# Gated attention with a token mixer: the accumulating stores taken out, four adds put on GpSimd, a clear put on VectorE, and a PSUM bank taken later

## The chip, the core and the metric

The kernel runs on one core of a Trainium2 chip. The core has a matrix engine (TensorE, in the rows PE, with its weight loads as PEld), three engines for elementwise work (VectorE, DVE in the rows; ScalarE, ACT; GpSimd, POOL), and a queue engine (SyncE, SP) that issues most transfers between HBM and the on-chip memory. GpSimd can issue transfers too. Matrix products go into PSUM, which has eight banks of 128 partitions by 512 fp32 numbers; everything else on the chip is in SBUF. The engines run side by side, each in the order of its own instructions, and wait for each other through semaphores.

The metric is the device time of one execution in microseconds (us). The kernel before takes 1622.77 us, the median of three runs (1622.52 to 1623.23).

## The reference

The input x has 2048 tokens of 512 numbers. It is normalised, and two branches work on the result, which are multiplied and added to x:

```python
xn = _layernorm(x)
s = attention(xn, wqkv, wo)          # 32 heads of 16, softmax over all 2048 tokens, then @ wo
g = silu(mixer(xn, w1, b1, w2, b2))  # layernorm, then an MLP across tokens: 2048 -> 1792 -> 2048, gelu
return x + s * g
```

All of it is fp32. A number is split into an upper and a lower part, and a product is made of three matrix products (upper by upper, upper by lower, lower by upper).

## The kernel before, in words

The tokens are 16 blocks (`b`) of 128. The kernel first normalises x and makes queries, keys and values; then comes the long middle part, in which the attention of one pair of heads after another goes through TensorE (scores, then exponentials on ScalarE, then the products with the values), while the maxima of the next pair's scores are found on VectorE. In the same loop stands a second stream of products, the filling: first all products of the mixer, then those of the output projection with `wo`. A step of the loop has an `s`; from `s = NU = 512` on there are no more maxima, and only scores, values and filling remain. The last heads end shortly before the end of the program, and the projection of the blocks 8 to 15 needs them, so it is completed after the loop.

**The filling.** A generator yields one product after another, and `take(n, each)` asks it for `n` of them and hands each to `each`. A generator step that begins a block also takes a PSUM bank for it (`ps_sc.hold("dn")`), and one that begins a quarter of a mixer weight also issues the weight's load and its split into two parts (`w_load`, `w_split`, on SP and GpSimd). After its `n` products, `take` looks at the next thing in the stream with `fill.peek()`, to see whether a block has ended. Looking at it makes it: the bank is taken, or the load and the split are issued, at this place in the program. The blocks 12 and 13 (`LATE` and the one after) are interleaved by three products each while `n < ND - 2`, so their banks are asked for in the same place.

**Banks.** Up to `s = 512` the scores have four banks (`ps_sc`), those of the maxima three (`ps_mx`). From then on all seven form one row: a tile takes the bank at the front and puts it to the back, a held bank leaves the row until it is given back. The scores of a step that follow each other take the row's banks in turn, and a score has to wait until the exponential that reads its bank is done.

**The last half of the blocks.** For each block from 8 on, the part of the projection that does not need the last heads is multiplied by g and added to x before the loop ends (`part`, then `store_y`). The result lies in HBM until the end: blocks 10 to 13 in the buffer `y_d`, from which `load_second` reads it back into `ys[b]`. The blocks 8 and 9 (`SUMMED`) are stored straight to the output.

**The end of the program.** After the loop, the last heads' numerators are turned by TensorE, divided on VectorE into `apart[0]` (a buffer that `clear_apart` sets to zero at `s = NU + 16`) and turned back. Then eight blocks are completed in the order 8, 9, 12, 13, 10, 11, 14, 15, which the code counts as `n = 0` to `7`. `product(n)` makes three matrix products; `gated(n)` multiplies them by g on VectorE; `added(i, eng)` adds `ys` and issues the store on SP. For the blocks 8 and 9 `added` issues an accumulating transfer on GpSimd's queue instead (`accum_op=OP.add`), which adds to what lies in the output. The dictionary `adding` says after which `n` each `added` stands. Block 15 goes by halves (`in_parts`).

Blocks 0 to 7 were completed before, inside the loop, by `finish` on VectorE.

Of the kernel before, what the change touches and what calls it, by code (L numbers as in the profile page):

```python
# [12 lines left out]
OP = mybir.AluOpType  # L13
# [9 lines left out]
def tile_attention_token_mixer(ctx, tc, x, wqkv, wo, w1, b1, w2, b2, out):  # L23
    nc = tc.nc
    P = 128
# [5 lines left out]
    NB = S // P  # L31
# [835 lines left out]
    apart = []  # L867

    def clear_apart():

        apart.append(el.tile([P, 2, 512], F32, name="uo"))
        nc.gpsimd.memset(apart[0], 0.0)

    xts = {}
    gts = {}
# [1 line left out]
    gates = {}  # L877
    held = []
    PARTS = NB - 2
    LATE = NB - 4  # L880
    HALVES = 5
    SUMMED = range(NB // 2, NB // 2 + 2)

    def load_part(b):

# [23 lines left out]
        after(2, two)  # L909

    def store_y(b, y):
        if b in SUMMED:
            nc.sync.dma_start(out[b * P : (b + 1) * P, :], y)
            return
        nc.sync.dma_start(y_d[b], y)
        if b >= NB // 2:
            unkept.append(b)
# [3 lines left out]
    def load_second():  # L921

        b = next((b for b in unkept if b >= PARTS), min(unkept))
        unkept.remove(b)
        i = b - NB // 2
        while len(held) < NB // 8:
            held.append(big.tile([P, S], F32, name="big"))
        ys[b] = held[i // 4][:, i % 4 * 512 : i % 4 * 512 + 512]
        nc.sync.dma_start(ys[b], y_d[b] if b < PARTS else xv[:, b, :])
# [110 lines left out]
    def everything():  # L1040
        yield from mixer()
        yield from rest()

    class Fill:
# [10 lines left out]
        def next(self):  # L1055
            x = self.peek()
            self.ahead.clear()
            return x

    fill = Fill(everything())  # L1060
    open_ = True
# [7 lines left out]
    def take(n, each):  # L1069

        nonlocal open_, done
        got = 0
        while open_ and (got < n or fill.peek() and len(fill.peek()) == 2):
            x = fill.next()
            if x is False:
                open_ = False
            elif x is None:
                break
            elif len(x) == 2:
                def then(empty, back):  # L1080
                    empty()
                    back()

                each(None, lambda x=x: then(*x))
                if fill.peek() is None:
                    fill.next()
                    break
            else:
                each(x, None)
                got += 1  # L1090
        done += got

    def whole(x, then):
# [279 lines left out]
    for c in range(2):  # L1373
        for a in range(2):
            j = 2 * a + c
            nc.vector.tensor_tensor(
                out=spread[:, c, :, 96 + DH * a : 112 + DH * a], in0=turned[:, :, j, DH * a : DH * a + DH],
# [12 lines left out]
    def lower(h, c):  # L1390
        o = oc[ND - 1, 2 + c][96:, :, 256 * h : 256 * h + 256]
        sub(nc.vector, o[:, 1, :], back[h, c][96:, :256], o[:, 0, :])
# [17 lines left out]

    def added(n, eng):
        b = half[n]
        if b in SUMMED:
            nc.gpsimd.dma_start(out[b * P : (b + 1) * P, :], gates[b], accum_op=OP.add)
            return
        eng.tensor_tensor(out=gates[b], in0=ys[b], in1=gates[b], op=OP.add)
        nc.sync.dma_start(out[b * P : (b + 1) * P, :], gates[b])

# [18 lines left out]
        turn_back(1, c)  # L1437
        upper(1, c)
    lower(1, 0)
    adding = {0: [0], 1: [1], 3: [2], 4: [3], 5: [4], 6: [5, 6]}  # L1440
    for n in range(8):
        if n > 5:
            some(len(beside) if n == 7 else len(beside) - 9)
        product(n)
        if n == 7:
            in_parts(n)
            break
        gated(n)
        for i in adding.get(n, ()):
            added(i, nc.gpsimd if i in () else nc.vector)  # L1450
        if n == 1:
            lower(1, 1)

# [26 lines left out]
```

## Time and profile before

| | us |
|---|---|
| median of three runs | 1622.77 |
| the profiled execution | 1621.93 |
| its span, from the first to the last instruction | 1620.0 |
| TensorE busy (11,899 products) | 1610.4 |
| VectorE busy | 1414.3 |
| ScalarE busy | 1192.3 |
| GpSimd busy | 552.4 |

The profile is of one execution. A row of the timeline has the start in us from the span's start, the duration in us, the engine, the line of the kernel, the operation, the tiles (written <- read), the shapes, how often, and in brackets the idle time of the engine before it with what ended it. A row of the windows has a stretch, and for each engine the busy time and in brackets the number of instructions, then the granted TensorE clock, the busy share of the DMA engines and the GB/s that they moved. A row of the chain of waits has a start, a duration and the work that the end of the program hung on at that time. A busy TensorE is not necessarily at its peak, since its products are pipelined: products of 512 columns follow each other every 0.23 us though each row shows 0.39.

### The profile page before, as it was taken

To read this page: it belongs to the slowest core of one execution; us is meant where nothing else is said; L and a number is where in the kernel's file an instruction comes from. 1 tells how busy PE (TensorE), PEld (TensorE's weight loads), DVE (VectorE), ACT (ScalarE), POOL (GpSimd) and SP (SyncE) were. 2 spreads that over 40 slices of the span, in tenths; PEclk is the share of its full clock that TensorE was granted. 3 is DMA by queue.
4 is the path that set the end of the run, shared out by engine and by line. 5 is a ranking of instruction groups with operands and counts; after the bars stand their busy time and mean duration, and the time that the engine had idled before them with its cause. 6 is when DMAs were issued, how large, how long until landed. Compare 5 with 4: busy or idle time off the path is not lost.

```text
span 1620.0 us, 31089 instructions
## 1 busy us (share of the span) xinstructions
PE 1610.4 (99%) x11899; PEld 876.2 (54%) x11899; DVE 1414.3 (87%) x2478; ACT 1192.3 (74%) x2306; POOL 552.4 (34%) x651
## 2 busy tenths in 40 slices
PE   9999999999999999999999999999999999999998
PEld 8888854554555554554454554544555545554544
DVE  7665999999999999999999999999999999999945
ACT  3333477777777777777877787777877777888885
POOL 1224844342244332332333332223232322563330
PEclk9999999999999999999999999999999999999999
DMA  7478441515133141826151522304150614444346
GB/s 231 178 249 200 120 93 41 96 39 78 41 68 75 27 79 40 241 71 109 41 83 37 85 59 42 69 31 76 38 86 31 113 32 80 112 99 131 111 136 222
DMA packets 151120, 153.34 MB, mean 95 GB/s; under 512 B 51372, under 2 KB 109996, under 8 KB 147900
## 3 DMA queue, kind: packets, MB, share of 16 engines
q1 hardware_dynamic: 146524, 150.25, 38.6%
q0 software_dynamic: 4448, 1.12, 0.5%
q8 instruction: 93, 1.52, 0.4%
q14 instruction: 55, 0.45, 0.1%
HBM read 99.63 MB, written 50.58 MB: 93 GB/s over the span
## 4 chain that ended last, share of the span: by engine, by line
PE 97%; DVE 1%; POOL 0%; issue 0%; ACT 0%; DMA 0%; SPq 0%; POOLq 0%; DVEq 0%
PE av L987 31%; PE dn L1132 23%; PE sc L971 17%; PE mx L533 14%; PE sc L436 3%; PE dn L672 2%; PE mx L436 2%; DVE mxp L537 1%; PE av L436 1%; PE dn L1178 0%; PE sc L104 0%; PE sc L102 0%; PE sc L103 0%; PE mx L340 0%; PE mx L102 0%; PE mx L104 0%
## 5 line engine op out<-in xcount | busy, mean ns | idle before, releaser
L537 DVE TENSOR_REDUCE mxp<-mx 128x1 f32<-128x512 f32 x2026 | 1250.3, 682 | 112.0 <-PE mx L533 85.7
L976 ACT ACTIVATE prob<-sc 128x512 f32<-128x512 f32 x2004 | 1039.7, 607 | 282.3 <-PE sc L971 116.5
L533 PE MATMUL mx<-big 48*128 48x512 f32 x2026 | 769.5, 419 | 0.1
L971 PE MATMUL sc<-big 50*128 50x512 f32 x2004 | 733.6, 412 | 0.5 <-ACT prob L976 0.5
L987 PE MATMUL av<-prob,vp 128*32 128x512 f32 x4096 | 545.5, 604 | 0.3 <-DVE ev L723 0.2
L1132 PE MATMUL dn<-hu,wh 64*128 64x512 f32 x1520 | 506.2, 404 | 0.0
L971 PEld LDWEIGHTS sc<-big 50*128 50x128 f32 x2004 | 353.9, 186 | 230.4 <-ACT prob L976 205.6
L533 PEld LDWEIGHTS mx<-big 48*128 48x128 f32 x2026 | 356.7, 185 | 196.0 <-DVE mxp L537 173.8
L1132 PEld LDWEIGHTS dn<-hu,wh 64*128 64x128 f32 x1520 | 272.1, 184 | 68.2 <-issue 45.3
L1132 PE MATMUL dn<-hu,wl 64*128 64x512 f32 x762 | 301.9, 396 | 0.0
L987 PEld LDWEIGHTS av<-prob,vp 128*32 128x32 f32 x4096 | 80.9, 108 | 176.3 <-issue 164.0
L95 POOL TENSOR_TENSOR wl<-raw,wh 128x512 fp32r<-128x512 f32 x124 | 150.7, 1218 | 64.0 <-ACT wh L167 22.6
L165 POOL CAST wh<-raw 128x512 fp32r<-128x512 f32 x104 | 60.4, 581 | 277.0 <-PE dn L1132 114.5
L1132 PEld LDWEIGHTS dn<-hu,wl 64*128 64x128 f32 x762 | 140.5, 184 | 11.6
L561 POOL CAST m<-f 16x128 fp32r<-16x128 f32 x31 | 8.7, 280 | 240.7 <-DVE f L549 240.7
L99 POOL DMA_DIRECT2D big<-m x124 | 65.6, 536 | 0.0
L622 POOL TENSOR_TENSOR sq<-u 128x512 f32<-128x512 f32 x11 | 11.5, 1041 | 133.7 <-ACT u L616 133.7
L1132 PE MATMUL dn<-wh,hu 64*128 64x512 f32 x144 | 51.0, 407 | 0.0
L709 POOL TENSOR_SCALAR t<-t 128x512 f32<-128x512 f32 x16 | 23.8, 1488 | 79.6 <-ACT t L706 79.5
L436 PE MATMUL sc<-xt,big 128*128 128x512 f32 x184 | 44.5, 390 | 0.0
L95 POOL TENSOR_TENSOR hu<-hx,hu 128x512 fp32r<-128x512 f32 x16 | 20.4, 1294 | 68.5 <-ACT hu L279 68.5
L672 PE MATMUL dn<-hu,wh 64*128 64x512 f32 x128 | 42.3, 392 | 0.0
(224 smaller groups left out, 1180.6 us busy)
## 6 DMA issues: line engine op xcount, KB each, us to landing
raw<-in_B_w_dram SPq DMA_DIRECT2D x104, 256.0 KB
big<-k_d SPq DMA_DIRECT2D x96, 128.0 KB
big<-q_d SPq DMA_DIRECT2D x96, 128.0 KB
q_d<-sg SPq DMA_DIRECT2D x16, 512.0 KB
k_d<-sg SPq DMA_DIRECT2D x16, 512.0 KB
num_d<-ev SPq DMA_DIRECT2D x30, 256.0 KB
u_d<-uo SPq DMA_DIRECT2D x14, 512.0 KB
hu<-u_d SPq DMA_DIRECT2D x14, 512.0 KB
```

The lines of the kernel that those rows point to most:

```text
L95: eng.tensor_tensor(out=o, in0=a, in1=b.bitcast(F32), op=OP.subtract)
L99: queue.dma_start(dst.bitcast(F32), src.bitcast(F32))
L165: nc.gpsimd.tensor_copy(whs[n][:, :m, :], raws[n][:, :m, :])
L436: nc.tensor.matmul(ps, w[part][:, kd, m], xt[kd][:, z, :], start=w is wh and z == 0 and kd == 0, stop=w is wl and kd == ND - 1,)
L533: nc.tensor.matmul(ps, q[o : o + 48, r * P : (r + 1) * P], k[o : o + 48, c * 512 : (c + 1) * 512], start=True, stop=True,)
L537: nc.vector.tensor_reduce(mxp[u // 16][:, a, r % 8, c : c + 1], ps, axis=AX.X, op=OP.max)
L672: nc.tensor.matmul(ps, w(slice(0, 64)), m(slice(0, 64)), start=first, stop=last)
L709: nc.gpsimd.tensor_scalar(t, t, 1.0, None, op0=OP.add)
L971: nc.tensor.matmul(ps, ks[p][o : o + 50, kb * P : (kb + 1) * P], qs[p][o : o + 50, at : at + 512], start=True, stop=True,)
L976: nc.scalar.activation(e, ps, AF.Exp, scale=scale)
L987: nc.tensor.matmul(av[32 * j : 32 * j + 32, :], vps[p][:, kb, 16 * a : 16 * a + 32], prob.pop((t, a, c)), start=kb == 0, stop=kb == NB - 1,)
L1132: made.append(lambda r=r, start=first and a == lead, stop=last and a != lead: nc.tensor.matmul(ps, w(r), m(r), start=start, stop=stop,))
```

## The change

It has five pieces.

1. `SUMMED` goes. The blocks 8 and 9 are stored to `y_d` and read back like the blocks 10 to 13, and there are no more accumulating transfers.
2. `added` for `n = 0` to `3` (blocks 8, 9, 12 and 13) is done by GpSimd, the rest by VectorE, and the adds stand at other places.
3. The clear of `apart[0]` is done by VectorE.
4. `take` looks at the next thing in the stream only behind the last product of a block (`x[4]` is the mark of the last product). Otherwise a bank is taken, and a weight's load and split are issued, in the next call of `take`, with the first product that they are for.
5. `while not held or ...` gives the same number of buffers as before at this size.

```diff
     def clear_apart():
         apart.append(el.tile([P, 2, 512], F32, name="uo"))
-        nc.gpsimd.memset(apart[0], 0.0)
+        nc.vector.memset(apart[0], 0.0)
...
-    SUMMED = range(NB // 2, NB // 2 + 2)
...
     def store_y(b, y):
-        if b in SUMMED:
-            nc.sync.dma_start(out[b * P : (b + 1) * P, :], y)
-            return
         nc.sync.dma_start(y_d[b], y)
         if b >= NB // 2:
             unkept.append(b)
...
-        while len(held) < NB // 8:
+        while not held or len(held) < NB // 8:
...
         got = 0
-        while open_ and (got < n or fill.peek() and len(fill.peek()) == 2):
+        ended = False
+        while open_ and (got < n or ended and fill.peek() and len(fill.peek()) == 2):
             x = fill.next()
...
             else:
                 each(x, None)
                 got += 1
+                ended = x[4]
...
     def added(n, eng):
         b = half[n]
-        if b in SUMMED:
-            nc.gpsimd.dma_start(out[b * P : (b + 1) * P, :], gates[b], accum_op=OP.add)
-            return
         eng.tensor_tensor(out=gates[b], in0=ys[b], in1=gates[b], op=OP.add)
         nc.sync.dma_start(out[b * P : (b + 1) * P, :], gates[b])
...
-    adding = {0: [0], 1: [1], 3: [2], 4: [3], 5: [4], 6: [5, 6]}
+    adding = {0: [0], 1: [1], 2: [2], 3: [3], 5: [4, 5], 6: [6]}
...
         for i in adding.get(n, ()):
-            added(i, nc.gpsimd if i in () else nc.vector)
+            added(i, nc.gpsimd if i < 4 else nc.vector)
```

What this does to the order of the instructions is seen at three places. The lines of the changed kernel have slightly smaller numbers: L1407 is the multiply that was L1409, L1411 the add that was L1416, L1418 and L1419 the halves of block 15.

VectorE at the end of the program, before, from the multiply of block 12 on (`prob<-sc` and `prob<-dn` are the multiplies, `prob<-big` the adds):

```order
L1409 TENSOR_TENSOR prob<-sc,hu 128x512 x2
L1416 TENSOR_TENSOR prob<-big,prob 128x512
L1409 TENSOR_TENSOR prob<-sc,hu 128x512
L1416 TENSOR_TENSOR prob<-big,prob 128x512
L1409 TENSOR_TENSOR prob<-sc,hu 128x512
L1416 TENSOR_TENSOR prob<-big,prob 128x512
L1409 TENSOR_TENSOR prob<-dn,hu 128x512
L1416 TENSOR_TENSOR prob<-big,prob 128x512 x2
L1423 TENSOR_TENSOR prob<-dn,hu 128x256
L1424 TENSOR_TENSOR prob<-big,prob 128x256
```

And in the changed kernel:

```order
L1407 TENSOR_TENSOR prob<-sc,hu 128x512 x4
L1411 TENSOR_TENSOR prob<-big,prob 128x512 x2
L1407 TENSOR_TENSOR prob<-dn,hu 128x512
L1411 TENSOR_TENSOR prob<-big,prob 128x512
L1418 TENSOR_TENSOR prob<-dn,hu 128x256
L1419 TENSOR_TENSOR prob<-big,prob 128x256
```

VectorE has five adds before and three after; the four multiplies of blocks 12, 13, 10 and 11 now follow each other.

GpSimd at the end of the program, the changed kernel's difference:

```order
-L905 TENSOR_TENSOR t<-t,xt 128x512 x3
-L872 MEMSET uo 128x1024
-L1414 DMA out_dram<-prob 128x512 x2
-L1476 UNCONDITIONAL_BRANCH
-L1476 ISA
+L904 TENSOR_TENSOR t<-t,xt 128x512 x3
+L1411 TENSOR_TENSOR prob<-big,prob 128x512 x4
+L1471 UNCONDITIONAL_BRANCH
+L1471 ISA
```

The clear has gone to VectorE (it stands there between the completions of blocks 3 and 4), and four adds stand where two accumulating transfers stood.

TensorE at the first products of block 13, two rounds of scores behind `s = 512`, before, with the tiles' numbers, which count up in the order in which tiles are taken. `sc` are scores, `dn_22597` is the bank of block 12 and `dn_22598` that of block 13:

```order
L971 MATMUL sc_22660<-big_1481,big_1482 128x512
L1178 MATMUL dn_22597<-wh_20255,hu_20596 128x512
L971 MATMUL sc_22665<-big_1481,big_1482 128x512
L1178 MATMUL dn_22597<-wl_20256,hu_20596 128x512
L1178 MATMUL dn_22598<-wh_20255,hu_20596 128x512
L1178 MATMUL dn_22597<-wh_20255,hu_20596 128x512
L1178 MATMUL dn_22598<-wl_20256,hu_20596 128x512
```

And in the changed kernel, where the two banks are `dn_22599` and `dn_22661`:

```order
L967 MATMUL sc_22662<-big_1481,big_1482 128x512
L1176 MATMUL dn_22599<-wh_20255,hu_20596 128x512
L967 MATMUL sc_22667<-big_1481,big_1482 128x512
L1176 MATMUL dn_22599<-wl_20256,hu_20596 128x512
L1176 MATMUL dn_22661<-wh_20255,hu_20596 128x512
L1176 MATMUL dn_22599<-wh_20255,hu_20596 128x512
L1176 MATMUL dn_22661<-wl_20256,hu_20596 128x512
```

The products stand in the same order. Block 13's bank is taken right behind block 12's before (22597, 22598), ahead of the second and the third score at `s = 512`, and two rounds later in the changed kernel, next to the score beside its own first product (22661, 22662).

In the middle part the same piece of the change moves some weight splits on GpSimd and loads on SP a few rows down, behind the small transfers of the maxima or the stores of g; on TensorE, VectorE and ScalarE the middle part's instructions stand as they stood.

## The prediction

> **What bounds the kernel now.** I read the windows first, for each stretch the busy time of the five engines.
>
> ```profile
> 20.00:1400.00 1380.00, 1379.93 (x10249) 756.37 (x10247) 1227.32 (x2144) 1008.48 (x1946) 467.34 (x560) 1.00 0.37 85
> ...
> 1560.00:1600.00 40.00, 39.83 (x296) 16.31 (x295) 14.98 (x24) 36.72 (x74) 3.45 (x3) 1.00 0.70 230
> ...
> 1606.00:1613.00 7.00, 6.61 (x30) 5.13 (x28) 6.87 (x12) 0.00 (x0) 1.86 (x2) 1.00 0.32 55
> ```
>
> TensorE (first number behind the length) has no gap in the middle part, 1379.93 of 1380.00 us, and almost none up to 1600 us. In the last stretch VectorE (third) is as full, 6.87 of 7.00. The chain of waits says who hands over to whom at the end:
>
> ```profile
> 1605.34 0.71 PE av L1403 x3
> 1606.07 0.72 DVE prob L1409 x2
> ...
> 1615.19 0.43 DVE prob L1424
> ```
>
> From 1606.07 us the end hangs on VectorE alone, up to the last half of block 15 at 1615.62. Behind it lie 4.4 us of transfer and closing. So the change can gain in two places: a stall of TensorE ahead of 1606 us, or the 14 us behind it. It can lose nearly anywhere that TensorE is made to wait.
>
> **The middle part: nothing.** TensorE, VectorE and ScalarE keep their order there; what moves is the split of some weight quarters on GpSimd, and loads on SP.
>
> ```profile
> POOL wh L165 <- PE dn L1132: 114.5, 16, 13.6
> ...
> L95 POOL TENSOR_TENSOR wl<-raw,wh 128x512 fp32r<-128x512 f32 x124 | 150.7, 1218 | 64.0 <-ACT wh L167 22.6
> ```
>
> The split mostly waits for TensorE to give a buffer back, up to 13.6 us; it is early, not late, and TensorE's list of waits names no split. A split that comes some rows later, behind a 0.3 us cast and four small transfers, uses up some of this. TensorE has no idle time to win and no wait on GpSimd, so I take 0, with 0.3 us either way for the range; if that cover were gone, each late split would cost TensorE up to its 1.2 us.
>
> **The bank: -0.4 us.** At `s = 512` TensorE stands still once:
>
> ```profile
> 1550.39 0.50 PE L971 MATMUL sc<-big 50*128 50x512 f32 x1 [0.49 <-ACT prob L976]
> ...
> 1549.74 1.78 ACT L976 ACTIVATE prob<-sc 128x512 f32<-128x512 f32 x3 [0.58 <-PE sc L971]
> ...
> 1548.75 0.68 DVE L898 TENSOR_TENSOR t<-dn,gt 128x512 f32<-128x512 f32 x1
> ```
>
> Blocks 12 and 13 both hold one of the scores' four banks, so the third score needs the bank of the first, whose exponential has just begun (1549.74). With block 13's bank still in the row, the second score goes to that bank, which VectorE had read by 1549.43, and the third to one that is free. All 0.49 us go at best. The fourth score then takes the first one's bank, free at about 1550.35, 0.1 us later than it could start, so I take 0.4; the lower end is 0, if another wait takes its place. From there to 1600 us TensorE is the fuller engine (39.83 of 40.00 against ScalarE's 36.72), so what is won here arrives at the end.
>
> **Stores and loads of blocks 8 and 9: nothing.** The two stores go to `y_d` in place of the output, and two loads of 256 KB come on SP. SP works in order, and the load of block 9 must wait until its store, issued at 1536.96, has landed.
>
> ```profile
> 1536.96 0.45 SPq L913 DMA_DIRECT2D out_dram<-t  x1
> ...
> 1549.44 0.34 SPq L889 DMA_DIRECT2D xt<-in_A_x_dram  x1
> ```
>
> The next entry in the queue goes out 12 us later for a reason of its own (the buffer it fills is in use). A store takes about 2 us to land (below), so the queue is free again by 1540.
>
> **The clear on VectorE: nothing.** It stands between the completions of blocks 3 and 4.
>
> ```profile
> 1579.58 0.95 POOL L872 MEMSET uo<- 128x1024 f32 x1
> ...
> 1590.12 0.69 DVE L956 TENSOR_TENSOR t<-hu,t 128x512 f32<-128x512 f32 x1
> 1591.70 0.69 DVE L955 TENSOR_TENSOR t<-dn,hu 128x512 f32<-128x512 f32 x1 [0.89 <-PE dn L1178]
> ```
>
> VectorE idles 0.89 us at that place and again before each following block. A clear of 1024 columns costs it between 0.95 (GpSimd's) and 1.4 us (twice a 512-column operation); block 4's completion is up to 0.5 us late and the next gap takes it up. Nobody waits for that bank at once, since seven go round.
>
> **The adds: +0.3 us on VectorE.** This is its end:
>
> ```profile
> 1607.94 1.29 DVE L1409 TENSOR_TENSOR prob<-sc,hu 128x512 f32<-128x512 f32 x2
> ...
> 1612.14 0.69 DVE L1409 TENSOR_TENSOR prob<-dn,hu 128x512 f32<-128x512 f32 x1
> 1612.74 1.29 DVE L1416 TENSOR_TENSOR prob<-big,prob 128x512 f32<-128x512 f32 x2
> 1613.94 0.42 DVE L1423 TENSOR_TENSOR prob<-dn,hu 128x256 f32<-128x256 f32 x1
> ...
> 1609.05 0.39 PE L1403 MATMUL sc<-wh,hu 128*128 128x512 f32 x1
> ...
> 1611.32 0.39 PE L1403 MATMUL dn<-wh,hu 128*128 128x512 f32 x1
> ...
> 1612.22 0.39 PE L1403 MATMUL dn<-wh,hu 128*128 128x512 f32 x1
> ```
>
> Operations of 512 columns follow each other every 0.60 us (1612.14, 1612.74), and from block 15's first half to the end it is 1.68 us (1613.94 to 1615.62). All times in this part are those of the profile, ahead of the 0.4. If nothing is in the way, the multiplies start at 1607.94, 1608.54, 1609.14 and 1609.74 (block 11's product is ready at 1609.44), the two adds at 1610.34 and 1610.94, block 14's multiply at 1611.75 (TensorE is done at 1611.71), its add at 1612.35, the halves at 1612.95. The end is 1614.63, 0.99 us earlier.
>
> But GpSimd adds at the same time, and such pairs are in the trace:
>
> ```profile
> 14.58 1.29 POOL L95 TENSOR_TENSOR big<-wh,big 128x512 fp32r<-128x512 f32 x1
> 15.62 0.81 DVE L95 TENSOR_TENSOR big<-wl,big 128x512 fp32r<-128x512 f32 x1
> 16.34 0.68 DVE L95 TENSOR_TENSOR big<-raw,big 128x512 fp32r<-128x512 f32 x1
> ...
> 1551.38 1.28 POOL L95 TENSOR_TENSOR hu<-sq,hu 96x512 fp32r<-96x512 f32 x1
> 1552.63 1.26 POOL L905 TENSOR_TENSOR t<-t,xt 128x512 f32<-128x512 f32 x1
> ...
> 1551.87 2.11 DVE L561 CAST m<-f 16x128 fp32r<-16x128 f32 x1
> ...
> 1548.13 1.28 POOL L905 TENSOR_TENSOR t<-t,xt 128x512 f32<-128x512 f32 x1
> 1548.75 0.68 DVE L898 TENSOR_TENSOR t<-dn,gt 128x512 f32<-128x512 f32 x1
> ...
> 1574.76 1.28 POOL L905 TENSOR_TENSOR t<-t,xt 128x512 f32<-128x512 f32 x1 [20.87 <-DVE t L898]
> ```
>
> A multiply with one input in PSUM and one in SBUF is not disturbed (0.68 beside GpSimd). A VectorE operation with both inputs in SBUF that began inside GpSimd's took 0.81, and its follower started 0.47 us after GpSimd's end (14.58 + 1.29 = 15.87; 16.34). A small cast was held for 2.11 us, through two GpSimd operations, to 1553.98. So the two adds of blocks 10 and 11, whose inputs are both in SBUF, are likely held. GpSimd's adds take 1.25 us each in a row (1551.38, 1552.63) and start 0.1 us after VectorE's result (the last row: VectorE's operation ended at 1574.69). Block 8's multiply ends at 1606.07 + 0.69 = 1606.76, so they end at 1606.84 + 3 x 1.25 + 1.28 = 1611.87. Block 10's add, wanted at 1610.34, waits for that; block 11's starts at 1612.34, and the rest follows by 0.60: 1612.94, 1613.54, halves 1614.14, end 1615.82, 0.2 later than before. If VectorE slips in between GpSimd's third and fourth add, block 11's add waits for the fourth, and the end is 1615.72. If GpSimd's adds stand 1.36 apart, it is 1616.15. I take +0.3 from bounds of -0.99 and +0.5, nearer the upper, since the cast's row shows a hold through two operations.
>
> A rule of the Trainium skill bears on this (SBUF — State Buffer, section Who interferes with whom): a VectorE instruction with two SBUF inputs and a GpSimd instruction that reads SBUF exclude each other, the one that comes first has the port for all its length, and one SBUF input doesn't contend. The row of 0.81 alone would say 0.13 us for each held add, thus -0.99 + 0.26 = -0.73 and 1620.4 in the end; by the rule the add stands still until GpSimd is done. No row has two GpSimd adds against two VectorE adds, so the trace agrees only in part.
>
> **The end of the transfers: -1.2 us.**
>
> ```profile
> 1609.85 4.81 SPq L1417 DMA_DIRECT2D out_dram<-prob  x5
> ...
> L1425 SPq DMA_DIRECT2D out_dram<-prob x2: 606/845/1084, 1614.8 to 1616.0; - x2
> ...
> 1610.01 1.86 POOL L1414 DMA_DIRECT2D out_dram<-prob  x2 [29.47 <-DVE prob L1416]
> ...
> 1610.40:1611.50 1.10, 1.10 (x6) 0.93 (x5) 1.10 (x3) 0.00 (x0) 1.10 (x2) 1.00 0.65 238
> 1611.50:1616.60 5.10, 1.11 (x5) 0.57 (x4) 4.05 (x9) 0.00 (x0) 0.37 (x1) 1.00 1.06 222
> 1616.60:1618.40 1.80, 0.00 (x0) 0.00 (x0) 0.00 (x0) 0.00 (x0) 0.00 (x0) 0.77 1.02 381
> 1618.40:1618.70 0.30, 0.00 (x0) 0.00 (x0) 0.00 (x0) 0.00 (x0) 0.00 (x0) 0.50 0.28 92
> 1618.70:1620.00 1.30, 0.00 (x0) 0.00 (x0) 0.00 (x0) 0.00 (x0) 0.00 (x0) 0.50 0.00 0
> ```
>
> The first store, issued at 1609.85, moves alone: 238 GB/s over 1.1 us are its 262 KB, landed by 1611.6, 1.75 us after its issue. Then the DMA engines are full (1.06) at only 222 GB/s while the accumulating transfers run, against 381 GB/s in the 1.8 us after them. The first half of block 15 takes 1.08 us to issue, so the second, ready at 1615.62, is issued at 1616.03 and lands by 1618.7, 2.65 later. Without the accumulating transfers (issued from 1610.01) the stores start 1.7 us earlier (GpSimd's first add ends at 1608.12), and most come further apart than the 0.69 us that 262 KB take at 381 GB/s. So the last should be issued at once, 0.03 behind VectorE as the first half is (-0.35), and land in 1.75 (-0.9). I take 1.2; the bounds are 0 and -1.3.
>
> The sum is 0 - 0.4 + 0 + 0 + 0.3 - 1.2 = -1.3 us. Against the profiled execution, 1621.93 (span 1620.0 and 1.9 around it), that is 1620.6; the runs' median is 0.84 above that execution, and 1622.77 - 1.3 gives **1621.5**.
>
> **Rivals.** *The adds of the two engines don't meet*: VectorE gains its 0.99, the sum is -0.4 - 1.0 - 1.2 = -2.6, 1620.2. For it speaks that 0.81 is little above 0.68; against it the cast of 2.11.
>
> *The transfers give nothing*: SP issues in order, and the stores of blocks 10 and 11 stand behind GpSimd's block 13 at 1611.9 or later; the stores crowd behind it and the last lands 2.6 us after its issue as before. Then -0.4 + 0.3 and -0.2 of the issue are left: 1622.5. Against it: from block 13 on four blocks are left, at 381 GB/s 2.8 us, and they have 4.
>
> *Slower, by one mechanism*: GpSimd's adds hold VectorE's multiplies too, and the engines take turns. From 1606.84, four adds of 1.28 with a multiply of 0.47 between bring block 10's multiply to an end at 1612.1, the fourth add to 1613.38, block 11's multiply and the adds behind it to 1616.38 for the halves, the end to 1618.06: +2.4 - 0.4 - 1.2 = +0.8, 1623.6. It decides if a multiply is held for over 0.3 us. The 0.68 of L898 beside two GpSimd operations speaks against it.
>
> *The bank moves nothing* is inside the forecast's range.
>
> **Chances and range.** Forecast 0.58 (its own range 1620.8 to 1622.2), no meeting 0.2, transfers 0.13, slower 0.05, anything else 0.04. Measured against no change, 0.2% is 3.2 us, which is about what a measurement of this kernel can tell. No case lies under 1619.5; with the spread of the second and half of the rest I give faster 0.09, slower (over 1626.0) 0.03, same 0.88. The range 1619.9 to 1622.8 takes in the second and third case and leaves out the slower one.
>
> **What would show it.** TensorE's idle 0.49 at 1550 gone; VectorE's adds of blocks 10 and 11 far above 0.69 each, starting or ending at the end of a GpSimd add, the multiplies at 0.69; the last issue right behind VectorE's last operation, and the DMA engines no longer full ahead of it. It is wrong if the middle part ends at another time, if VectorE waits in the clear, or if SP stands behind the load of block 9.

## The result, and the profile after

| | before | after |
|---|---|---|
| median, us | 1622.57 (14 runs) | 1625.28 (14 runs) |
| the profiled execution | 1621.93 | 1626.54 |
| its span | 1620.0 | 1624.8 |

The medians are 2.7 us apart: the change makes the kernel slower, where 1.3 us less had been forecast. The ratio is 1.0019 (it would be 3.1 us), with a 95% interval of 1.0012 to 1.0026. That is less than the 0.2% up to which the prediction called the time the same, but the sign is the other one and the time lies outside the range.

The parts that the prediction priced came out near their forecast sizes. The stall of TensorE at `s = 512` is gone; these are the timeline's scores there and the windows around them, in the changed kernel:

```profile
1549.08 0.68 PE L967 MATMUL sc<-big 50*128 50x512 f32 x2
1550.69 1.05 PE L967 MATMUL sc<-big 50*128 50x512 f32 x3
```

```profile
1540.00:1560.00 20.00, 20.00 (x153) 8.80 (x149) 15.22 (x26) 16.27 (x33) 10.10 (x9) 1.00 0.43 141
```

The three scores follow each other with no idle time in brackets, and TensorE is busy for 20.00 of 20.00 us. The clear stands in a gap of VectorE and takes 0.91 us; the gap behind the next block is still 0.90 us long:

```profile
1592.03 0.91 DVE L872 MEMSET uo<- 128x1024 f32 x1 [0.16 <-issue]
...
1595.11 0.69 DVE L951 TENSOR_TENSOR gt<-dn,gt 128x512 f32<-128x512 f32 x1 [0.90 <-PE dn L1176]
```

At the end of the program, VectorE, GpSimd and the stores (timeline of the changed kernel):

```profile
1607.13 0.69 DVE L1407 TENSOR_TENSOR prob<-av,hu 128x512 f32<-128x512 f32 x1
...
1609.01 2.48 DVE L1407 TENSOR_TENSOR prob<-sc,hu 128x512 f32<-128x512 f32 x4
1611.42 2.58 DVE L1411 TENSOR_TENSOR prob<-big,prob 128x512 f32<-128x512 f32 x2
...
1616.48 0.42 DVE L1419 TENSOR_TENSOR prob<-big,prob 128x256 f32<-128x256 f32 x1
...
1607.96 5.48 POOL L1411 TENSOR_TENSOR prob<-big,prob 128x512 f32<-128x512 f32 x4 [27.25 <-DVE prob L1407]
...
1609.27 6.41 SPq L1412 DMA_DIRECT2D out_dram<-prob  x7
1616.14 1.12 SPq L1420 DMA_DIRECT2D out_dram<-prob  x2
```

The four multiplies run at the usual pace beside GpSimd (2.48 us for four, 0.60 apart). The two adds of the blocks 10 and 11 are held, 2.58 us for two in place of 1.29, but only the second of them until GpSimd is through with its four. Here are GpSimd's third and fourth add and VectorE's two, one by one (timeline of the changed kernel in narrow windows):

```profile
1610.45 1.29 POOL L1411 TENSOR_TENSOR prob<-big,prob 128x512 f32<-128x512 f32 x1
...
1611.70 1.74 POOL L1411 TENSOR_TENSOR prob<-big,prob 128x512 f32<-128x512 f32 x1
...
1611.42 0.88 DVE L1411 TENSOR_TENSOR prob<-big,prob 128x512 f32<-128x512 f32 x1
...
1612.22 1.77 DVE L1411 TENSOR_TENSOR prob<-big,prob 128x512 f32<-128x512 f32 x1
```

VectorE's first add begins inside GpSimd's third, ends some 0.55 us behind it, and so gets in ahead of the fourth, which takes 1.74 us in place of 1.29. The second ends some 0.55 us behind the fourth.

From the start of block 8's multiply to the end of VectorE it is 9.77 us (1607.13 to 1616.90), before 9.55 (1606.07 to 1615.62): 0.22 longer, for a forecast of 0.3. The last store is issued as VectorE ends, at 1616.93, and the last packet lands at 1618.46. From block 8's multiply that is 11.33 us in place of 12.58.

So all data lie in the output by 1618.5, about as early as before (1618.65), and the program ends at 1624.8. What fills the rest stands in no list of busy times. The rows of the kernel's last line, which hold what each engine does at its close (median and longest duration in ns, first and last start in us), are these in the kernel before:

```profile
L1476 POOLq DRAIN  x3: 46/108/6888, 1610.5 to 1619.7; - x3
L1476 SPq DRAIN  x3: 7/7/13, 1619.1 to 1619.4; - x3
```

and in the changed kernel:

```profile
L1471 POOLq EVENT_SEMAPHORE  x4: 17/17/17, 1624.0 to 1624.7; - x4
L1471 POOLq DRAIN  x3: 46/102/13577, 1610.4 to 1624.5; - x3
L1471 SPq DRAIN  x3: 7/7/13, 1619.2 to 1624.2; - x3
```

Of the windows of the changed kernel, the last one:

```profile
1619.30:1624.00 4.70, 0.00 (x0) 0.00 (x0) 0.00 (x0) 0.00 (x0) 0.00 (x0) 0.50 0.00 0
```

Each engine closes with a DRAIN and a round of semaphores. GpSimd's first DRAIN ran from 1610.47 to 1617.35 before (1610.5 + 6.89), and nobody saw it, since SP was through at 1619.2. In the changed kernel it runs from 1610.41 to 1623.99, 10.55 us behind the end of GpSimd's last add (1613.44), while SP was through at 1619.28. In the window, 4.7 us long, nothing runs on any engine and no transfer moves. These 4.7 us are more than the whole loss.

### The profile page after: what moved, and what is told of

Same layout as the page of the kernel before. It is cut to its first block, busy times and chain, and to the rows that moved or that the text cites. A ratio compares the mean times of both kernels' runs of the same rounds, so it can differ in the third digit from the quotient of the medians.

```text
span 1624.8 us, 31087 instructions
## 1 busy us (share of the span) xinstructions
PE 1611.3 (99%) x11899; PEld 874.6 (54%) x11899; DVE 1416.1 (87%) x2477; ACT 1192.2 (73%) x2306; POOL 553.6 (34%) x652
## 3 DMA queue, kind: packets, MB, share of 16 engines
q0 software_dynamic: 4160, 0.60, 0.3%
## 4 chain that ended last, share of the span: by engine, by line
PE 98%; DVE 1%; DMA 0%; ACT 0%; issue 0%; SPq 0%; POOL 0%; ACTq 0%; DVEq 0%
PE av L983 31%; PE dn L1130 24%; PE sc L967 16%; PE mx L533 14%; PE sc L436 3%; PE dn L672 3%; PE mx L436 2%; PE av L436 1%; PE sc L102 0%; PE sc L104 0%; PE sc L103 0%; PE mx L967 0%; DMA raw<-in_A_wqkv_dram 0%; PE mx L102 0%; PE dn L1176 0%; PE mx L104 0%
```

## The experiments

Theory at the start: the program can close only some 10.5 us after GpSimd's last operation. Rivals: the length depends on how much or what GpSimd did last; or the loss sits in another piece of the change. All ratios are against the kernel before, run beside it on the same chip (medians 1622.1 to 1622.6).

### Where the loss sits: four runs

All seven whole adds on VectorE (e1):

```diff
-            added(i, nc.gpsimd if i < 4 else nc.vector)
+            added(i, nc.vector)
```

> The changed kernel with all seven whole adds on VectorE; GpSimd's last operation is then the add of block 7, some 30 us before the end. Theory (the program cannot close until about 10.5 us after GpSimd's last operation, when GpSimd's closing DRAIN ends): the DRAIN is over long before the stores are. VectorE has four adds of 0.60 us more and no add that is held, so in the changed kernel's own time it ends at 1607.13 + 14 x 0.60 + 0.38 + 1.68 = 1617.6 (0.7 later than with GpSimd's help), the last store lands by 1619.4, and the span is 1620.5 to 1620.9, about 4 us less than the 1624.8 of the changed kernel: a time of about 1621.3, 0.9 to 1.3 below the kernel before if the carry-over of 1 us in the middle part is chance, equal to it if it is not. Rival (the loss sits elsewhere: in the middle part, the clear, or the stores and loads of blocks 8 and 9): the span stays at 1624 to 1625.5 and the time at 1625 to 1626. Rival (closing takes that long whenever no transfers stand on GpSimd's queue): the DRAIN is as long and the span also stays.

Measured: 1622.28 us, ratio 0.9999 (0.9991 to 1.0008), span 1620.4. The loss is in GpSimd's adds; the bank, the clear and the stores of the blocks 8 and 9 don't carry it. That the time is not below that of the kernel before, as expected if the late start of the tail is chance, comes from the tail itself: VectorE ends 11.28 us behind the start of block 8's multiply (1606.15 to 1617.43), where the expectation has 10.5. An add right behind the multiply of its own block starts some 0.72 us after it and not 0.60. GpSimd's last operation then ends at 1579.71, and its DRAIN is as long as ever, only early (closing line of this run):

```profile
L1471 POOLq DRAIN  x3: 46/102/11861, 1578.4 to 1620.1; - x3
```

1578.40 + 11.86 = 1590.26, again 10.55 us behind the last operation.

Two adds on GpSimd (e2, `i < 2`):

> The changed kernel with two adds (blocks 8 and 9) on GpSimd in place of four. Theory (a fixed 10.5 us behind the last operation): GpSimd's last add ends near 1610.5, its DRAIN at 1621.1, the span is 1621.9, 2.9 less than the changed kernel, time about 1623.6 to 1623.9 with the VectorE end at 1617.6 hidden behind it. Rival (the closing is proportional to the work, 10.5 us for four adds, 2.6 for each): the DRAIN ends at 1615.8 and hides, the stores decide, span 1620.7. Rival (the length comes from the fourth add that VectorE broke into): as the proportional one, or with the DRAIN as before, 5.5 us behind the last operation. Rival (loss elsewhere): 1624 to 1625.

Measured: 1622.73 us, 1.0003 (0.9994 to 1.0012). The last add ends at 1609.18 in this execution, 1.3 us earlier than I had put it since the whole tail starts earlier; the DRAIN ends at 1619.73, 10.55 behind it, and sticks out 1.2 us behind SP, through at 1618.55. Neither the number of adds nor the fourth one that VectorE broke into matters.

The bank alone, on the kernel before (e3):

```diff
-        while open_ and (got < n or fill.peek() and len(fill.peek()) == 2):
+        ended = False
+        while open_ and (got < n or ended and fill.peek() and len(fill.peek()) == 2):
...
                 got += 1
+                ended = x[4]
```

> The kernel before with one piece of the change: the look at the next thing in the stream only behind a block's last product. The idle 0.49 us of TensorE at the third score at s = 512 goes. If the 1 us by which the changed kernel was late at 1526 us is chance of the one profiled execution, the time is 0.4 to 0.5 us below the kernel before; if it comes from the splits and loads that this piece moves, 0.5 us above it. In both cases GpSimd's DRAIN is about 5.5 us behind its last transfer's issue and hides.

Measured: 1622.16 us, 1.0000 (0.9991 to 1.0009). The time can't tell half a microsecond from nothing, but the windows can; ahead the kernel before, then this run:

```profile
1540.00:1560.00 20.00, 19.51 (x147) 8.87 (x145) 13.52 (x24) 16.10 (x33) 10.04 (x9) 1.00 0.32 102
```

```profile
1540.00:1560.00 20.00, 20.00 (x151) 8.96 (x151) 14.23 (x25) 16.35 (x33) 10.09 (x9) 1.00 0.33 103
```

A tiny late copy on GpSimd, in the kernel before (e4):

```diff
+            if i == 6:
+                nc.gpsimd.tensor_copy(sm.tile([P, 1], F32, name="dot", bufs=1), gates[half[6]][:, :1])
```

> The kernel before with one tiny operation more: GpSimd copies one column (128x1) of block 14's finished sum into a tile that nobody reads; it can start when VectorE has added block 14, at about 1614.0. No other engine has anything to wait for. Theory (a fixed 10.5 us behind GpSimd's last operation, whatever its size): the DRAIN ends at 1614.2 + 10.5 = 1624.7 and the span is 1625.5, 5.5 us more than before: a time of about 1628. Rival (the closing grows with GpSimd's last work): a column is nothing, the DRAIN ends 5.5 us behind it, 1619.7, the span grows by 0.5. Rival (loss elsewhere): no change, 1622.6.

Measured: 1622.53 us, 1.0001 (0.9992 to 1.0010), where the theory had 1628. The theory of a fixed length falls here (the copy in the timeline, then the closing line):

```profile
1615.24 0.19 POOL L1452 COPY dot<-prob 128x1 f32<-128x1 f32 x1 [2.22 <-DVE prob L1416]
```

```profile
L1478 POOLq DRAIN  x3: 46/108/3031, 1615.2 to 1620.6; - x3
```

The DRAIN ends at 1618.26, 2.8 us behind the copy.

### Not the kind of the last operation: four runs

My next theory was that a copy as the last operation is cheap and an add dear. The changed kernel with a one-column copy behind GpSimd's fourth add (e5):

```diff
+            if i == 3:
+                nc.gpsimd.tensor_copy(sm.tile([P, 1], F32, name="dot", bufs=1), gates[half[3]][:, :1])
```

> The changed kernel with one operation more: behind its fourth add GpSimd copies one column (128x1) of block 13's sum into a tile that nobody reads. So far the closing DRAIN ended 10.55 us behind GpSimd's last operation where that was an add of two tiles (the changed kernel, with two adds, and with none late: 10.54 to 10.55), and 2.82 us behind it where it was the copy of a column. Theory (the kind of GpSimd's last operation sets the length): the DRAIN ends 2.8 us behind the copy, near 1616.5 in the changed kernel's own time, hidden behind the stores; the span is 1620.0 in place of 1624.8, and the time 1.0 us (tail) and 0.5 us (bank) below the kernel before, 1621. Rival (10.5 us must pass from the last add of two tiles, whatever follows, or the operation behind it waits so long): the DRAIN or the copy ends at 1624 and the span stays at 1624.8. Rival (proportional to the last operation's size) gives the same as the theory here and is told apart by the next run.

Measured: 1625.65 us, 1.0021 (1.0012 to 1.0030). The copy ends at 1612.59, the DRAIN at 1623.13, 10.54 later.

The kernel before with a late one-column add in place of e4's copy (e6):

> The kernel before with the same late place as the earlier late copy, but an add of two columns (128x1) in place of the copy of one. Theory (kind): the DRAIN ends 10.5 us behind it, near 1624.9, 5.5 us behind the stores: span 1625.5, time near 1628, ratio 1.0034. Rival (size): as with the copy, 2.8 us, hidden, no change of the time.

Measured: 1622.37 us, 1.0001 (0.9992 to 1.0010); the DRAIN ends 3.5 us behind the add. The changed kernel with a memset last (e7):

> The changed kernel with a memset of 128x1 on GpSimd behind its fourth add, in place of the copy. Which kinds are short isn't known: if only an operation that reads two tiles is long, the DRAIN ends about 2.8 us behind it and the span is 1620; if the copy is the exception, 10.5 us and 1624.8.

Measured: a span of 1624.3 (one time, 1626.10), the DRAIN 10.55 us behind the memset. The theory of the kind falls with all three. What parts the two groups is what the queue of GpSimd does: in all kernels made from the one before, accumulating transfers are under way at the end, and the DRAIN ends 0.76 to 0.78 us behind their last packet (packet and end of the DRAIN: 1616.58 and 1617.35 before, 1616.98 and 1617.74 in e3, 1617.48 and 1618.26 in e4, 1617.59 and 1618.37 in e6).

The fourth run (e8) asks why VectorE's adds are held. On top of e5, the products of the blocks 10, 11 and 14 are written into their own PSUM bank:

```diff
-        gates[b] = pp.tile([P, 512], F32, name="prob")[:, :D]
+        if n < 4:
+            gates[b] = pp.tile([P, 512], F32, name="prob")[:, :D]
+        else:
+            gates[b] = sums[b]
...
-        eng.tensor_tensor(out=gates[b], in0=ys[b], in1=gates[b], op=OP.add)
-        nc.sync.dma_start(out[b * P : (b + 1) * P, :], gates[b])
+        to = gates[b] if n < 4 else pp.tile([P, 512], F32, name="prob")[:, :D]
+        eng.tensor_tensor(out=to, in0=ys[b], in1=gates[b], op=OP.add)
+        nc.sync.dma_start(out[b * P : (b + 1) * P, :], to)
```

> The changed kernel with the copy behind GpSimd's fourth add, and with the products by g of the blocks 10, 11 and 14 written in place into PSUM, so that VectorE's adds of these blocks read one tile of SBUF and one of PSUM. If VectorE's adds were held because both of their tiles lie in SBUF, like GpSimd's, nothing is held now: four multiplies from 1609.01 at 0.60 us, two adds to 1612.6, block 14 from 1612.8 (TensorE) to 1614.0, the halves to 1615.7, 1.2 us earlier than the 1616.90 of the changed kernel; the span is 1618.8, the time 2.7 us below the kernel before (1.0 tail, 1.2 this, 0.5 bank), 1619.7, ratio 0.9983. Rival (any VectorE add is held beside GpSimd's, or PSUM makes the operations slower by 0.2 us or more each): VectorE ends at 1616.7 to 1617 and the time is that of the run with the copy alone.

Measured: 1624.88 us, 1.0017 (1.0008 to 1.0026). The time is still that of the long DRAIN, but VectorE is as expected (timeline):

```profile
1608.73 1.29 DVE L1410 TENSOR_TENSOR sc<-sc,hu 128x512 f32<-128x512 f32 x2
1609.93 1.27 DVE L1415 TENSOR_TENSOR prob<-big,sc 128x512 f32<-128x512 f32 x2
1611.35 0.70 DVE L1410 TENSOR_TENSOR dn<-dn,hu 128x512 f32<-128x512 f32 x1 [0.15 <-PE dn L1401]
...
1606.48 5.04 POOL L1415 TENSOR_TENSOR prob<-big,prob 128x512 f32<-128x512 f32 x4 [27.26 <-DVE prob L1410]
```

The two adds take 1.27 us in place of 2.58, beside GpSimd's third and fourth; GpSimd's own take 5.04 in place of 5.48. VectorE now waits 0.15 us for TensorE and ends 8.70 us behind the start of block 8's multiply, against 9.77.

### What shortens the DRAIN: four runs

The store of block 13 on GpSimd's own queue, else the changed kernel (e9):

```diff
-        nc.sync.dma_start(out[b * P : (b + 1) * P, :], gates[b])
+        (nc.gpsimd if n == 3 else nc.sync).dma_start(out[b * P : (b + 1) * P, :], gates[b])
```

> The changed kernel with the store of block 13 on GpSimd's own queue in place of SP's. The runs so far fall into two groups: where no transfer of GpSimd's queue was under way (the changed kernel, two adds, none late, a copy or a memset last) the DRAIN ended 10.54 to 10.55 us behind GpSimd's last operation, whatever that was; in the kernel before and the three made from it the DRAIN ended 0.76 to 0.78 us behind the last packet of the accumulating transfers of GpSimd's queue, whatever stood last. Theory (with a transfer of its queue still under way the closing ends with the transfer, without one it takes 10.5 us): the store goes out at 1613.5 to 1614.5 in the changed kernel's time, lands near 1616.3, the DRAIN ends at 1617.1 and hides; the span is 1620.0 in place of 1624.8, the time 1.5 us below the kernel before (1.0 tail, 0.5 bank). Rival (10.5 us behind the last operation here too; the two groups differ by the accumulating): the DRAIN ends at 1625, span 1625.8, time 1627.

Measured: 1620.92 us, 0.9991 (0.9982 to 1.0000). One line, and the 4.7 us in which nothing runs are gone (the store's issue in the timeline, then the closing line):

```profile
1616.04 0.65 POOL L1412 DMA_DIRECT2D out_dram<-prob  x1 [3.23 <-issue]
```

```profile
L1471 POOLq DRAIN  x3: 40/112/3062, 1616.0 to 1619.6; - x3
L1471 SPq DRAIN  x3: 7/7/13, 1618.9 to 1619.3; - x3
```

The DRAIN ends at 1619.08, 0.72 us behind the store's last packet (1618.36) and only 0.06 behind SP, through at 1619.01. What I had not foreseen is the 3.23 us ahead of the issue, in which GpSimd waits for nothing that the profile shows.

That store and the PSUM products together (e10):

> The changed kernel with the store of block 13 on GpSimd's queue, and with the products of the blocks 10, 11 and 14 written in place into PSUM. With the PSUM products alone VectorE ended 8.70 us behind the start of block 8's product (9.55 before, 9.78 in the changed kernel), and SP was through 11.72 us behind it (13.13 before). Theory: the DRAIN hides, SP's end decides, 1.4 us earlier than before, and 0.5 from the bank: 1.9 us below the kernel before, ratio 0.9988, below 1 with its whole interval. Rival (the DRAIN isn't shortened): as the last run, 1625, ratio 1.0017 to 1.002.

Measured: 1620.31 us, 0.9988 (0.9979 to 0.9997): its whole interval lies below the kernel before.

One small transfer of GpSimd's queue between its adds, in the changed kernel (e11):

```diff
+            if i == 0:
+                nc.gpsimd.dma_start(y_d[half[0]][:, :1], gates[half[0]][:, :1])
```

> The changed kernel with a small transfer (one column of block 8's sum, 512 bytes, to a row of the scratch buffer that nobody reads again) on GpSimd's queue behind its first add; it lands while the three other adds run. Theory (only a transfer that is under way when the DRAIN begins shortens it): the DRAIN ends 10.5 us behind the last add, which comes 1 us later than in the changed kernel: span 1625.5 to 1626. Rival (a transfer shortly before is enough): the DRAIN hides, span near 1620.5.

Measured: a span of 1622.2 (one time, 1623.95). The transfer had landed at 1612.59, GpSimd's last add ends at 1615.55, and the DRAIN at 1616.30, 0.75 behind it. So the transfer need not be under way: the rival is right. The time is lost elsewhere, since the issue again costs 3.23 us, GpSimd's three other adds come that much later, and one add of VectorE is held through all three of them, 3.87 us in place of 0.69 (timeline):

```profile
1611.17 0.65 POOL L1447 DMA_DIRECT2D y_d<-prob  x1 [3.23 <-DVE prob L1411]
1611.84 3.71 POOL L1411 TENSOR_TENSOR prob<-big,prob 128x512 f32<-128x512 f32 x3
...
1612.24 3.87 DVE L1411 TENSOR_TENSOR prob<-big,prob 128x512 f32<-128x512 f32 x1
```

No transfer on GpSimd's queue in the whole program (e12):

```diff
-            nc.gpsimd.dma_start(ks[p][row : row + 2, :].bitcast(F32), ones)
+            nc.sync.dma_start(ks[p][row : row + 2, :].bitcast(F32), ones)
...
-            eng, queue = (nc.gpsimd, nc.gpsimd) if u < NU - 1 else (nc.vector, nc.sync)
+            eng, queue = (nc.gpsimd, nc.sync) if u < NU - 1 else (nc.vector, nc.sync)
```

> The changed kernel with all 128 small transfers that GpSimd issues during the middle part (the negated maxima and the rows of ones) on SP's queue, so that GpSimd's queue has no transfer in the whole program. SP then waits for the maxima among its other transfers, so the middle part may get longer by some us; only the distance from GpSimd's last add to the end of the DRAIN counts. If the 10.5 us belong to GpSimd's queue (closing a queue that has been used), the DRAIN ends within 1 us of the add, and the span loses 4 us behind it. If they are the price of the DRAIN itself behind any work, they stay at 10.5.

Measured: one time of 1620.41, span 1618.6. Here are GpSimd's adds in the timeline, then the closing line:

```profile
1606.81 5.49 POOL L1411 TENSOR_TENSOR prob<-big,prob 128x512 f32<-128x512 f32 x4 [27.26 <-DVE prob L1407]
```

```profile
L1471 POOLq DRAIN  x3: 39/78/3099, 1609.3 to 1618.4; - x3
```

The DRAIN ends at 1612.36, 0.07 us behind the last add (1612.30). The 10.5 us are a price of GpSimd's queue, paid at the close.

### Time, or number of transfers: four runs

What does the queue pay for: that it rested since the last maxima at 1521, or the 128 small transfers that it had carried?

Only the 124 transfers of the maxima moved to SP (e14; the second edit of e12), so that four are left, all before 150 us:

> The changed kernel with the 124 transfers of the negated maxima on SP's queue; GpSimd's queue keeps the 4 transfers of the rows of ones in the first part of the program, over 1500 us before the end. If the closing pays for a queue that has been used at all and has rested, the DRAIN ends 10.5 us behind the last add (span 1623 to 1625). If it pays for the number of transfers that have gathered (10.5 us for 128, 0.08 each), it ends 0.4 us behind it and hides (span 1619 to 1620).

Measured: span 1618.6, one time of 1620.36. The closing line, then the queue's transfers in the list of issues:

```profile
L1471 POOLq DRAIN  x3: 40/102/3455, 1609.4 to 1618.3; - x3
```

```profile
big<-ones POOLq DMA_DIRECT2D x4, 16.0 KB, 6.6
```

The DRAIN ends at 1612.84, 0.43 us behind the last add, as by number, though the queue had rested for 1450 us. A rest alone costs little.

One small transfer meant to land some 6 us before the end of the adds (e15: behind the reciprocals), or to go out some 30 before it (e16: beside the clear), in the changed kernel:

```diff
+    nc.gpsimd.dma_start(y_d[half[0]][:, :1], rq[:, 0, :1])
...
+        nc.gpsimd.dma_start(y_d[0][:, :1], apart[0][:, 0, :1])
```

> The changed kernel with one small transfer of GpSimd's queue (512 bytes) at the start of the tail, behind the reciprocals, near 1601; it lands some 6 us before the DRAIN begins its own work. A small transfer that had landed 3 us before made the DRAIN end 0.75 us behind the last add. If a recent transfer is enough and 6 us is recent, the DRAIN hides: span 1619.5 to 1620.5. If the queue rests within 6 us, 10.5 us: span 1623.5 to 1625.

> The same with the small transfer beside the clear, some 25 to 40 us before the end. If what counts is that some transfer came after the long run of other work since the last maxima (1521), the DRAIN hides here too: span 1619.5 to 1620.5. If what counts is the time since the last transfer, and the queue rests within some 25 us, 10.5 us behind the last add: span 1623.5 to 1625.

Measured: spans of 1619.3 and 1619.0 (one time each, 1621.08 and 1620.77). The DRAIN ends 0.75 us behind the last add in both, at 1613.03 and 1613.14, though the transfers had landed at 1607.99 and 1599.28, so that 13 us of rest change nothing either. (Issued, they were later than I had put them, at 1606.57 and 1595.11.)

Together, the end of the DRAIN behind the later of GpSimd's last operation and its queue's last packet:

| transfers of GpSimd's queue | kernels | us |
|---|---|---|
| none | e12, e13 | 0.07 |
| 4, early | e14 | 0.43 |
| 128, the last at 1521 | after, e1, e2, e5, e7, e8 | 10.54 to 10.55 |
| 128, and one or two in the last 30 us | before, e3, e4, e6, e9, e10, e11, e15, e16 | 0.72 to 0.78 |

10.48 us for 128 transfers and 0.36 for 4 are 0.08 and 0.09 each; by packets (4160 and 192) it is 2.5 and 1.9 ns each, so these two numbers don't tell transfers from packets. That, and the 3.23 us that a late issue costs, suggest a queue on which work for finished transfers piles up until something uses the queue again or closes it. The runs show the lengths; that this is what GpSimd does in them is argued only, and the trace has something against it. In the middle part the queue is used again every 39 to 50 us, four transfers at a time, and none of these issues comes late or gets longer. Here is the last group of the kernel before, with no idle time in brackets (timeline):

```profile
1518.04 0.45 POOL L95 TENSOR_TENSOR m<-f,m 16x128 fp32r<-16x128 f32 x1
1518.44 2.10 POOL L99 DMA_DIRECT2D big<-m  x4
```

If each use settled what had piled up, four transfers would be left for the close, and not 128. The late issues stood behind 74 to 95 us without a transfer. What the queue settles when, and why one late transfer leaves 0.75 us, where by number it should leave less, stays open.

**The version that beats both** (e13): the changed kernel, without transfers on GpSimd's queue, and with the PSUM products.

> The changed kernel with no transfer on GpSimd's queue in the whole program and with the products of the blocks 10, 11 and 14 written in place into PSUM. Without GpSimd's transfers the DRAIN ended 0.07 us behind GpSimd's last add, and one execution took 1620.41. Theory: VectorE ends 8.7 us behind the start of block 8's product, SP is through 11.7 us behind it as in the first run with the PSUM products, GpSimd is through before that: the time is 1.9 to 2.3 us below the kernel before, ratio 0.9986 to 0.9988. Rival (SP, which then issues 128 more transfers and waits for the maxima, delays the middle part): 1622 or more.

Measured: 1619.66 us (11 runs), ratio 0.9982 (0.9973 to 0.9991). It is 2.9 us below the kernel before on the same chip (1.5 to 4.4 by the interval), where 1.9 to 2.3 were expected; the rival that SP's 128 further transfers delay the middle part didn't happen.

## Why the prediction was wrong, step by step

**The step that failed** is in its first part: "Behind it lie 4.4 us of transfer and closing". I took the closing as something that follows the last landing by a fixed time, and summed only what ends VectorE's work and the stores. GpSimd's DRAIN was no term. In the trace of before it was there to be read, 6.89 us long, with 1.9 us to spare. And the accumulating transfers, which the prediction counted only as traffic in the way of the stores, kept it short: with transfers of its queue at the end, GpSimd closed 0.77 us behind them; without any, 10.55 us behind its last add. An item that was removed had a second use. The sum -1.3 and the exposed 4.7 us (1623.99 against SP's 1619.28) make +3.4; measured are +2.7, with an interval of 1.9 to 4.2.

The other steps:

- *The middle part, 0*: right as far as it can be seen. The first pair of traces showed the end of the loop 1.06 us later, and I suspected the moved splits. The runs say it is chance: block 8's multiply starts at 1606.07, 1606.67 and 1607.22 in three executions of the body of before, and between 1605.66 and 1607.13 in eleven of the body after.
- *The bank, -0.4*: the idle 0.49 is gone in every profile with that piece, and the averages of those starts are 1606.65 and 1606.23, 0.42 apart, with a spread that is larger than that. Right, and too small for a time of its own (e3).
- *Stores and loads of the blocks 8 and 9, the clear: 0*. The price is right; e1 has both and is as fast as before. The working for the load of block 9 is not. The prediction let its store land in 2 us; in the changed kernel SP stood 7.1 us for it (the list of SP's waits from 1535 to 1560 us, then the store, the load and the next entry in SP's timeline):

```profile
SPq L925 <- DMA y_d<-t: 7.1, 1, 7.1
```

```profile
1538.93 0.43 SPq L911 DMA_DIRECT2D y_d<-t  x1
1546.55 0.32 SPq L925 DMA_DIRECT2D big<-y_d  x1
1551.37 0.33 SPq L888 DMA_DIRECT2D xt<-in_A_x_dram  x1
```

  It cost nothing, since the next entry went out at 1551.37 only, 4.5 us later.
- *The adds, +0.3*: 0.22 measured. The multiplies aren't touched and the adds are held, but by the side case and not by the main one: the first add got in ahead of GpSimd's fourth, for which the prediction's working has 0.1 (1615.72 in place of 1615.62), and not 0.2 (1615.82). Where the first add was held through the fourth (e15), VectorE ended 10.02 us behind the start of block 8's multiply, 0.47 later than before (with GpSimd's adds 0.09 us later than in the changed kernel). So each case was dearer than its working, and that +0.3 is near 0.22 is in part luck. In seven kernels (after, e5, e7, e9, e12, e14, e16) VectorE's add began 0.32 to 0.34 us before the end of a GpSimd add and got in ahead of the next; it was held on where it began 0.42 (e15) or 0.89 us before (e11). What decides isn't known. The row of 0.81, from which the prediction took 0.13 us for a held add, shows a full hold: that operation began 0.25 us before GpSimd's ended (15.62 and 15.87) and ended 0.56 behind it. The rival that VectorE's multiplies are held (1623.6) gave a time near the measured one by a mechanism that didn't happen. The rule cited from the Trainium skill (SBUF — State Buffer, section Who interferes with whom) holds here, where the prediction had only partial rows for it: an add with both inputs in SBUF stood still through three GpSimd adds (3.87 us in e11), and with one input in PSUM two adds took 1.27 us beside GpSimd's (e8).
- *The transfers, -1.2*: with the 0.22 of VectorE inside, the last landing came 1.25 us earlier and SP's end 1.0 (1619.21 - 1606.07 = 13.14 before, 1619.28 - 1607.13 = 12.15 after). The forecast for both terms was -0.9. Without the 0.22 the term itself is -1.2 by SP's end, as forecast, and -1.5 by the last landing, a little more than its bound of -1.3: the last store is issued 0.03 us behind VectorE and lands in 1.53 us, where 1.75 was taken. One sign failed: the DMA engines are still full ahead of that issue, though at 379 GB/s and not at 222 (windows of the changed kernel):

```profile
1614.40:1616.90 2.50, 0.00 (x0) 0.00 (x0) 2.40 (x6) 0.00 (x0) 0.00 (x0) 0.92 1.03 379
```

  In e9 the DRAIN hardly sticks out, and half of this gain remains (the DRAIN ends 12.57 us behind block 8's multiply, SP before at 13.14); with the bank's 0.4 that makes 1.0, and the time is 1.2 us lower. The rivals that the engines' adds don't meet and that the transfers give nothing are both refuted by these rows.

So the priced parts came out near their sizes, the adds by a side case, and the time was wrong by a part that had no price.

## What to carry to other kernels

The end of a program has a bound on every engine, GpSimd's close among them: read the rows of the kernel's last line for each engine's DRAIN, with its spare time, as a term of the sum. A queue of GpSimd that carried many transfers and then none made the close 10.5 us long here; keep GpSimd's last work more than that ahead of the end, give its queue a late transfer (which held GpSimd up for 3.2 us here), or move its small transfers to another queue. And when a change removes something, ask not only what it cost but what it kept going.

## What the runs showed of the hardware that I had not expected

- GpSimd's closing DRAIN: 0.07, 0.43, 0.75 or 10.55 us behind its last work, by what its queue had carried, and 10.54 to 10.55 alike behind an add of 512 columns (after), a copy of one column (e5) and a memset of one column (e7).
- The first transfer that GpSimd issued after 74 to 95 us without one came 3.23 us after it could (e9, e10, e11, e15, e16), and 3.25 us after block 8's multiply in the kernel before (1606.76 and 1610.01), where the profile names another releaser. In the middle part, after 39 to 50 us without one, the issue follows at once, and four in a row take 2.10 us in all.
- Writing a product in place into PSUM freed VectorE's next add from GpSimd at no cost that can be seen: 1.29 us for two such multiplies, as into SBUF.
- Executions whose bodies are the same reach the same instruction up to 1.5 us apart at 1606 us, while from there to VectorE's end those with the same tail agree within 0.02 (9.54 to 9.55 in four with the tail of before). Small differences are read inside the stage, not from the span's start.
